# Attention and two feed-forward blocks on one core: a seven-product scheme in all four matrix layers, with running sums seeded in PSUM

## The chip, the cores and the metric

The kernel runs on one core of a Trainium2 chip, as one launch. The metric is the device time in microseconds; the median of several runs counts. The core has five engines that run beside each other: TensorE (PE, matmuls, with its weight loads as PEld), VectorE (DVE), ScalarE (ACT), GpSimd (POOL) and SyncE (SP), which here issues nearly all DMAs. PSUM has eight banks into which TensorE writes; SBUF holds everything else on the core.

## The reference

```python
def _attn_ref(q, k, v, w_pre, w_post):            # 4 batches, 12 heads, 448 rows, 64 wide
    scores = np.matmul(q, k.transpose(0, 1, 3, 2)) / np.sqrt(64)
    scores = np.einsum('bhij,hg->bgij', scores, w_pre)
    attn = softmax over the last axis (with its maximum taken off)
    attn = np.einsum('bhij,hg->bgij', attn, w_post)
    return np.matmul(attn, v)

def _moe_ref(x, w_gate, w_val, w_out):            # x 1792 x 768, d_ff 1536
    gate = 1.0 / (1.0 + np.exp(-(x @ w_gate)))
    return (gate * (x @ w_val)) @ w_out

def _moe2_ref(x, w_in, w_out):                    # d_ff 2048
    h = np.maximum(x @ w_in, 0.0)
    return (h * h) @ w_out
```

The result of the attention, with its heads side by side, is the x of the first block, whose result is the x of the second.

## The kernel before

The attention part comes first and is written out by hand in `attention`. The feed-forward part is made by `mlp`, which lists tasks (a DMA, a split, a job of three matmuls, a sum) with the engines that can run them, the time they are needed by (counted in TensorE jobs) and the buffers they use. `Feed` is a planner: it holds durations for each kind of task and emits the tasks in the order that its own clock gives, some of them between the steps of the attention, the rest after it. The order on each engine is thus fixed when the kernel is built; on the chip each engine works through its own list and waits where data or a buffer isn't there.

The 1792 tokens are handled as two halves of two batches each. A half's activations are two column blocks of 448 tokens (c = 0, 1), and a matrix is cut into tiles of 128 x 128. There are four matrix layers: gv (gate and val together), wo, wi and wo2. The order is gv, wo for the first half, gv, wo for the second, then wi, wo2 for the first and wi, wo2 for the second. Every matrix product is done in higher precision by splitting both operands into a rounded part and a rest (`split`: a cast on ACT, a subtraction on DVE). One `job` multiplies one weight tile with one operand of 128 x 448 in three matmuls, so a layer's work is counted in jobs.

The layers gv and wi take two weight tiles by two in the contraction and in the output, with the two column blocks, as a 2 x 2 block product, and do it in seven products instead of eight (`quad`). `PRODUCTS = ("a1", "b6", "c7", "d5", "a2", "c4", "d3")` gives the order of the products and in which of four PSUM banks each is summed. ACT copies the first product out of its bank, and DVE forms the other running sums from the banks and SBUF buffers (`c`). The layers wo and wo2 are done with all eight products (`plain`): for three output tiles at a time, over the contraction, each weight tile is used for both column blocks, so the six tiles of one weight buffer serve twelve jobs.

Weights come from the host in a compressed 64-bit form. `convert` turns twelve tiles at a time into floats (`raw`: two ACT operations, two DVE operations and two GpSimd adds for each half), forms for gv and wi the three or four block sums of the seven-product scheme (on DVE or GpSimd, whichever the planner finds free) and stores the blocks to DRAM. `Stream.unit` later loads six tiles at a time (`w32`, three buffers) and splits them into `w` (three buffers). `PACE` and `BEFORE` set from which TensorE job on a piece of conversion may be emitted. Operands of gv and wi are loaded, combined and split in `operands`; for wo and wo2 each g tile is split into one of six short-lived buffers (`brief`) right before use.

Of the kernel before, what the change touches and what calls it, by code (L numbers as in the profile page):

```python
# [19 lines left out]
P = 128  # L20
# [11 lines left out]
GT3 = 3  # L32
# [424 lines left out]
BEFORE = 10  # L457
PACE = 44
PRODUCTS = ("a1", "b6", "c7", "d5", "a2", "c4", "d3")


def square_order(KT, MT):

    order = []
    for m in range(0, MT, 2):
        for dm, dk in ((0, 0), (0, 1), (1, 1), (1, 0)):
            order += [(k + dk, m + dm) for k in range(0, KT, 2)]
    return order


def plain_order(KT, MT):

    return [(k, m + i) for m in range(0, MT, GT3) for k in range(KT) for i in range(GT3)]

# [24 lines left out]
class Feed:  # L499
# [122 lines left out]
    def emit(self, at, t, o):  # L622
# [5 lines left out]
        if t.size:  # L628
            self.wire = max(self.wire, end) + t.size / 250e3
            end = self.wire + self.land  # L630
# [56 lines left out]
def mlp(ctx, tc, xs, wg, wv, wo, wi2, wo2, out):  # L687
# [10 lines left out]
    tiles = {"wg": wg, "wv": wv, "wo": wo, "wi2": wi2, "wo2": wo2}  # L698
    K1, K2 = wg.shape[0] * UT // KD, wi2.shape[0] * UT // KD
    W = UT * P  # L700
    H3 = KD // 2
    BL = H3 * P

# [14 lines left out]
    def after_mixes():  # L718
# [3 lines left out]
        feed.stock(xts, pool("m_x1", 1, side="left"), 1)  # L722
        feed.stock(banks, pool("m_ps0", 6, space=PSUM, side="left"), 6)

    def after_all():
# [3 lines left out]
        feed.stock(cs, pool("m_c", 2, side="left"), 2)  # L729
# [6 lines left out]


    pace = [-BEFORE]

    def convert(key, src, n, square, dst, need):  # L740

        hold = max(0, min(pace[0] * PACE, need))
        pace[0] += 1

        y = Buf(ys, [P, 8 * BL], F32, "y")

        def t(*a, **kw):
            feed.task(*a, **kw).hold = hold

        for h in range(2):  # L750
            raw = Buf(raws, [P, W, 2], U32, "raw")
            part = [(y, b) for b in ((0, 4), (5, 7))[h]] if square else [(y, 4 * h), (y, 4 * h + 1)]

            def at(h=h, y=y):
                v = y.tile.bitcast(U32)
                if square:
                    v = v.rearrange("p (b e) -> p b e", e=BL)
                    return v[:, (0, 5)[h] : (5, 8)[h] : (4, 2)[h]]
                return v[:, h * W : (h + 1) * W]

            def of(ap):
                return ap.rearrange("p (b e) -> p b e", e=BL) if square else ap

            def load(e, i, h=h, raw=raw):
                v = src[2 * n + h].bitcast(U32).rearrange("p (m t) -> p m t", t=2)
                e.dma_start(out=raw.tile[:, i * BL : (i + 1) * BL], in_=v[:, i * BL : (i + 1) * BL])

            def bias(e, raw=raw):
# [378 lines left out]
```

## Time and profile before

| | before |
|---|---|
| median of three runs | 1429.9 us |
| the runs | 1419.75, 1429.9, 1431.61 us |
| the profiled execution, its time and its span | 1432.88 and 1431.2 us |
| TensorE busy, matmuls | 1380.3 us (96%), 7848 |
| DVE, ACT, POOL busy | 1041.0 (73%), 699.1 (49%), 333.1 us (23%) |
| DMA | 259.85 MB, 182 GB/s |

The time is that of the whole execution on the device, the span runs from its first to its last instruction. Busy shares add up neither over engines nor over stages: an engine that idles may still be the one that is waited for.

### The profile page before, as it was taken

The page shows a single profiled execution, that of the slowest core. Times are in us where ns is not written, and L with a number is a line of the kernel's source. Part 1 is how long each engine was busy: PE and PEld are TensorE (multiplying, and loading weights), DVE is VectorE, ACT ScalarE, POOL GpSimd, SP SyncE. Part 2 cuts the span into 40 slices and gives each one's busy share as a digit, 9 for nine tenths or more (in the row PEclk, how much of TensorE's full clock was granted, in tenths as well). Part 3 has the DMA queues.
Part 4 walks back from the last instruction along what each step waited for, and adds up shares of the span by engine and source line. Part 5 has one row for each costly group of instructions (what it writes and reads, how often), then busy time and mean ns, then how long its engine had stood idle before and what let it go on. Part 6 is the DMA issues. An engine that isn't in the chain of part 4 may idle for free.

```text
span 1431.2 us, 22572 instructions
## 1 busy us (share of the span) xinstructions
PE 1380.3 (96%) x7848; PEld 1113.8 (78%) x7848; DVE 1041.0 (73%) x1864; ACT 699.1 (49%) x1312; POOL 333.1 (23%) x356
## 2 busy tenths in 40 slices
PE   6889998999999899999999999999999999999999
PEld 2445555565665689999898999999899999999998
DVE  2767777797797787789767778987879854666442
ACT  2444445455555544446654455566445644233353
POOL 3243443343352032131124222022212100000000
PEclk9999999999999999999999999999999999999999
DMA  5757868868768256655665666377665433333121
GB/s 152 209 187 213 243 184 250 246 197 256 236 188 274 90 189 225 221 178 172 209 231 191 231 229 207 99 266 261 217 192 167 167 106 103 103 109 88 56 83 39
DMA packets 123342, 259.85 MB, mean 182 GB/s; under 512 B 16156, under 2 KB 62684, under 8 KB 123228
## 3 DMA queue, kind: packets, MB, share of 16 engines
q1 hardware_dynamic: 122848, 257.83, 57.2%
q8 instruction: 62, 1.02, 0.3%
q10 hardware_dynamic: 380, 0.57, 0.1%
q14 instruction: 52, 0.43, 0.1%
HBM read 163.74 MB, written 55.05 MB: 153 GB/s over the span
## 4 chain that ended last, share of the span: by engine, by line
PE 85%; DMA 7%; DVE 5%; ACT 1%; issue 1%; POOL 1%; SPq 0%; DVEq 0%; POOLq 0%; ACTq 0%
PE ps L886 64%; PE ps_p L283 8%; PE ps_s L202 5%; PE ps_v L312 4%; PE ps_m L238 4%; DMA g<-e 4%; DMA vraw<-in_v 2%; DVE ap L295 1%; DVE nm L249 1%; DVE e L212 1%; DMA t<-xs 1%; DVE s L874 0%; DVE w L874 0%; POOL wn L267 0%; ACT e L214 0%
## 5 line engine op out<-in xcount | busy, mean ns | idle before, releaser
L886 PE MATMUL ps<-s,w 128*128 128x448 f32 x4536 | 933.0, 367 | 6.4 <-DVE s L874 3.1
L886 PEld LDWEIGHTS ps<-s,w 128*128 128x128 f32 x4536 | 851.9, 188 | 87.5 <-DVE s L874 5.7
L797 POOL TENSOR_TENSOR y<-y,raw 128x384 int32<-128x384 int32 x136 | 161.6, 1205 | 528.1 <-DVE y L781 171.0
L871 ACT CAST w<-w 128x768 fp32r<-128x768 f32 x196 | 163.3, 835 | 181.8 <-PE ps L886 155.1
L283 PEld LDWEIGHTS ps_p<-wn,a 128*112 128x112 f32 x1440 | 158.7, 178 | 89.2 <-POOL wn L267 38.6
L874 DVE TENSOR_TENSOR w<-w,w 128x768 fp32r<-128x768 f32 x196 | 207.4, 1061 | 26.7 <-ACT w L871 23.1
L874 DVE TENSOR_TENSOR s<-g,s 128x448 fp32r<-128x448 f32 x224 | 152.9, 699 | 99.2 <-ACT s L871 98.8
L871 ACT CAST s<-g 128x448 fp32r<-128x448 f32 x224 | 126.5, 567 | 166.5 <-PE ps L886 159.9
L283 PE MATMUL ps_p<-wn,a 128*112 128x120 f32 x1440 | 183.9, 276 | 11.9 <-POOL wn L267 5.5
L900 DVE TENSOR_TENSOR c<-ps,c 128x448 f32<-128x448 f32 x200 | 124.4, 622 | 90.3 <-PE ps L886 86.8
L267 POOL TENSOR_SCALAR wn<-wq,sm 128x120 f32<-128x120 f32 x166 | 115.3, 695 | 272.6 <-DVE sm L264 207.7
L249 DVE TENSOR_REDUCE nm<-ps_m 128x1 f32<-128x448 f32 x180 | 111.1, 617 | 54.0 <-PE ps_m L238 53.9
L256 ACT ACTIVATE a<-ps_m,nm 128x448 f32<-128x448 f32 x180 | 114.5, 636 | 57.1 <-DVE sm L261 45.6
L295 DVE COPY ap<-ps_p 112x480 f32<-112x480 f32 x180 | 114.4, 649 | 14.2 <-PE ps_p L283 12.8
L202 PE MATMUL ps_s<-k,q 64*120 64x448 f32 (+1 forms) x384 | 108.5, 627 | 15.3 <-ACT e L214 9.7
L214 ACT COPY e<-ps_s 120x448 f32<-120x448 f32 (+1 forms) x96 | 51.1, 532 | 130.3 <-PE ps_s L202 87.5
L238 PE MATMUL ps_m<-g,wp 64*64 64x448 f32 x720 | 93.5, 580 | 5.1 <-DMA g<-e 5.1
L212 DVE COPY e<-ps_s 120x448 f32<-120x448 f32 (+1 forms) x96 | 60.0, 625 | 50.9 <-PE ps_s L202 28.5
L312 PEld LDWEIGHTS ps_v<-ap,vraw 112*64 112x64 f32 x768 | 52.7, 137 | 49.7 <-ACT xo L327 13.7
L312 PE MATMUL ps_v<-ap,vraw 112*64 112x240 f32 (+1 forms) x768 | 82.7, 360 | 8.6 <-DMA vraw<-in_v 7.1
L202 PEld LDWEIGHTS ps_s<-k,q 64*120 64x120 f32 (+1 forms) x384 | 31.0, 184 | 61.5 <-ACT a L256 20.4
L908 ACT COPY c<-ps 128x448 f32<-128x448 f32 x88 | 46.5, 533 | 52.0 <-PE ps L886 49.3
(40 smaller groups left out, 684.2 us busy)
## 6 DMA issues: line engine op xcount, KB each, us to landing
w<-gv SPq DMA_DIRECT2D x84, 384.0 KB
g<-e SPq DMA_DIRECT2D x132, 210.0 KB
raw<-in_wo SPq DMA_DIRECT2D x56, 384.0 KB
w<-wo SPq DMA_DIRECT2D x56, 384.0 KB
w<-wi SPq DMA_DIRECT2D x56, 384.0 KB
gv<-y SPq DMA_DIRECT2D x36, 384.0 KB
raw<-in_wi SPq DMA_DIRECT2D x32, 384.0 KB
vraw<-in_v SPq DMA_DIRECT2D x48, 224.0 KB
```

The source lines that it names most:

```text
L202: nc.tensor.matmul(ps[o][:isz], lhsT=q_t[n][r, p, :isz], rhs=kt[r], start=True, stop=True)
L238: nc.tensor.matmul(ps[u * HP : (u + 1) * HP], lhsT=wp[r], rhs=g_t[n][r, 2 * t + u], start=True, stop=True,)
L249: nc.vector.tensor_reduce(out=nm, in_=ps, op=ALU.max, axis=AX.X, negate=True)
L267: nc.gpsimd.tensor_scalar(out=wn, in0=wq, scalar1=sm, scalar2=None, op0=ALU.mult)
L283: nc.tensor.matmul(ps[:JP, jt], lhsT=a[:, jt * JP : (jt + 1) * JP], rhs=wn.rearrange("p g i -> p (g i)"), start=True, stop=True,)
L295: nc.vector.tensor_copy(ap[c][:, :, :, g0 - i0 : g0 - i0 + rows], ps[:JP, :, :, :rows])
L312: nc.tensor.matmul(ps[o * D : (o + 1) * D, :w], lhsT=vraw[c, (h + o) // HV][:, (h + o) % HV, jt, :], rhs=ap[c][:, jt, h + o, :w], start=jt ...
L797: e.tensor_tensor(out=y3, in0=y3, in1=c3, op=ALU.add)
L871: e.copy(dst.tile[:, 0], src.tile)
L874: e.tensor_tensor(out=dst.tile[:, 1], in0=src.tile, in1=dst.tile[:, 0].bitcast(F32), op=ALU.subtract)
L886: e.matmul(bank.tile, lhsT=a[k], rhs=x[l], start=start and n == 0, stop=stop and n == 2, skip_group_check=more,)
L900: e.tensor_tensor(out=out.tile, in0=a.tile, in1=b.tile, op=op)
```

## The change

The layers wo and wo2 are now done in seven products as well (`deep`), over all pairs of the contraction for one product before the next is begun, for the three pairs of output tiles at once. All their weights have to be in place, as seven blocks instead of four, when the layer begins, and a weight buffer of six tiles serves six jobs. The subtractions of the scheme on the operand side are done on g tiles in SBUF (`first`, and in `deep`).

In all four layers the products come in another order, 1 5 6 2 7 3 4, and the running sums are kept in PSUM: when product 1 is done ACT copies its bank a into bank b, and product 6 is added to it by its matmuls; then b is copied into c, and products 7 and 4 are added there, and 3 is added into b. `wide` (gv, wi) runs two such quads side by side (gate and val, or two pairs of outputs), `deep` three. So that matmuls add to what ACT has written, `prime` lets a matmul write each of the eight banks once before the first layer.

The dependencies of a job on the cast and on the rest of a split are now kept apart. The planner's conversion pacing changes (`BEFORE`, `FAST`, `PACE`), it counts 330 instead of 250 bytes per ns for DMAs, there are three `c` buffers instead of two and twelve `t` buffers instead of thirteen, and converted blocks are stored in pieces of 1536 instead of up to 3072 bytes for each partition.

```diff
-BEFORE = 10
-PACE = 44
-PRODUCTS = ("a1", "b6", "c7", "d5", "a2", "c4", "d3")
+BEFORE = 11
+FAST = 22
+PACE = 36
+PRODUCTS = ("1a", "5d", "6b", "2a", "7c", "3b", "4c")
+SUMS = ((1, 7, 6, ALU.add), (2, 1, 0, ALU.subtract), (4, 0, 7, ALU.subtract), (5, 3, 2, ALU.subtract))
...
+    def prime(w, slot):
+
+        b = [Buf(banks, [P, N], F32, "ps") for _ in range(8)]
+
+        def run(e):
+            for x in b:
+                e.matmul(x.tile, lhsT=w[0].tile[:, 0, :P], rhs=slot.tile[:, 0], start=True, stop=True)
...
+    def quads(count, jobs, then):
+
+        a, d, b, c = ([Buf(banks, [P, N], F32, "ps") for _ in range(count)] for _ in range(4))
+        bank = {"a": a, "b": b, "c": c, "d": d}
+        p5, v = {}, {}
+        for n, (name, k) in enumerate(PRODUCTS):
+            jobs(n, name, bank[k], name in "15")
             now = len(feed.jobs)
...
+            for i in range(count):
+                if name == "1":
+                    activate(b[i], a[i], now - 1)
+                elif name == "5":
+                    p5[i] = temp()
+                    activate(p5[i], d[i], now)
+                elif name == "6":
+                    activate(c[i], b[i], now)
+                elif name == "2":
+                    then(i, 0, 0, a[i], now)
+                elif name == "7":
+                    v[i] = temp()
+                    tt(v[i], c[i], p5[i], ALU.add, now, False)
+                    then(i, 1, 1, v[i], now)
+                elif name == "3":
+                    tt(p5[i], b[i], p5[i], ALU.add, now, False)
+                    then(i, 0, 1, p5[i], now)
+                else:
+                    then(i, 1, 0, c[i], now)
...
+    def wide(stream, hf, pair, slot, then):
+
+        def jobs(n, name, bank, fresh):
+            for i in range(2):
+                for q in range(H3):
+                    w = stream.tile(hf, pair * PAIR + (2 * n + i) * H3 + q, len(feed.jobs))
+                    job(bank[i], w, slot[name, q], fresh and q == 0, q == H3 - 1, fresh)
+
+        quads(2, jobs, then)
+
+    def deep(stream, hf, g, then):
+
+        pairs = stream.pairs
+
+        def jobs(n, name, bank, fresh):
+            for j in range(pairs):
+                k = 2 * j
+                b11, b12, b21, b22 = g[k, 0], g[k, 1], g[k + 1, 0], g[k + 1, 1]
+                now = len(feed.jobs)
+                if name == "6":
+                    tt(b12, b22, b12, sub, now)
+                elif name == "7":
+                    tt(b11, b12, b11, sub, now)
+                elif name == "4":
+                    tt(b21, b21, b12, sub, now)
+                src = {"1": b11, "5": b12, "6": b12, "2": b21, "7": b11, "3": b22, "4": b21}[name]
+                s = Buf(brief, [P, 2, N], F32R, "s")
+                split(src, s, N, now)
+                for i in range(H3):
+                    w = stream.tile(hf, (n * pairs + j) * H3 + i, len(feed.jobs))
+                    job(bank[i], w, s, fresh and j == 0, j == pairs - 1, fresh)
+
+        quads(H3, jobs, then)
...
-    def plain(stream, hf, KT, g, then):
-
-        for m0 in range(0, KD, GT3):
...
-                for i in range(GT3):
-                    w = stream.tile(hf, (m0 * KT + k * GT3) + i, len(feed.jobs))
-                    for c in range(2):
-                        if k == 0:
-                            bank[i, c] = Buf(banks, [P, N], F32, "ps")
-                        job(bank[i, c], w, s[c], k == 0, k == KT - 1)
...
+    def first(g, p):
+        k = 2 * p
+        tt(g[k, 1], g[k, 1], g[k, 0], sub, len(feed.jobs) + 60)
```

Three places of the order show what moves. The names are the program's: `w` is a split weight buffer, `s` a split operand, `g` the gated or squared values, `t` operands of the next layer, `c` sums in SBUF, `ps` banks, `raw` and `y` conversions.

TensorE's list, from the end of the attention part on, before and then in the change:

```order
L238 MATMUL ps_m<-g_147,wp 64x448 x4
L283 MATMUL ps_p<-wn,a 112x120 x8
L238 MATMUL ps_m<-g_147,wp 64x448 x2
L283 MATMUL ps_p<-wn,a 112x120 x16
L312 MATMUL ps_v<-ap,vraw 64x208 x48
L886 MATMUL ps<-s,w 128x448 x4536
```

```order
L237 MATMUL ps_m<-g_135,wp 64x448 x4
L282 MATMUL ps_p<-wn,a 112x120 x8
L237 MATMUL ps_m<-g_135,wp 64x448 x2
L282 MATMUL ps_p<-wn,a 112x120 x16
L311 MATMUL ps_v<-ap,vraw 64x208 x48
L921 MATMUL ps<-s,w 128x448 x8
L903 MATMUL ps<-s,w 128x448 x4284
```

The attention part ends alike; eight priming matmuls are new, and 4284 matmuls of the layers stand where 4536 stood.

DVE's list in the first wo layer, from its third weight split on, before and then in the change (the number tells buffers apart):

```order
L874 TENSOR_TENSOR w_6856<-w32_6785,w_6856 128x768
L874 TENSOR_TENSOR s_6763<-t_5510,s_6763 128x448
L900 TENSOR_TENSOR t_5510<-t_5554,t_5510 128x448
L900 TENSOR_TENSOR t_6917<-t_5565,t_5510 128x448
L874 TENSOR_TENSOR s_6915<-g_6145,s_6915 128x448
L874 TENSOR_TENSOR s_6926<-g_6181,s_6926 128x448
L874 TENSOR_TENSOR w_6932<-w32_6799,w_6932 128x768
L874 TENSOR_TENSOR s_6938<-t_6917,s_6938 128x448
L900 TENSOR_TENSOR t_5554<-t_5565,t_5554 128x448
L874 TENSOR_TENSOR s_6953<-g_6166,s_6953 128x448
L874 TENSOR_TENSOR s_6959<-g_6137,s_6959 128x448
```

```order
L891 TENSOR_TENSOR w_6962<-w32_6874,w_6962 128x768
L891 TENSOR_TENSOR s_6971<-g_6850,s_6971 128x448
L891 TENSOR_TENSOR s_6981<-g_5717,s_6981 128x448
L928 TENSOR_TENSOR g_5717<-g_5689,g_5717 128x448
L928 TENSOR_TENSOR g_6929<-g_6929,g_6850 128x448
L928 TENSOR_TENSOR g_5632<-g_5717,g_5632 128x448
L891 TENSOR_TENSOR w_7003<-w32_6919,w_7003 128x768
L891 TENSOR_TENSOR s_7009<-g_5948,s_7009 128x448
L891 TENSOR_TENSOR s_7015<-g_6192,s_7015 128x448
L928 TENSOR_TENSOR g_5948<-g_5919,g_5948 128x448
L928 TENSOR_TENSOR g_6192<-g_6157,g_6192 128x448
```

Between two weight splits stand two operand splits and two or three subtractions on g, where before stood operand splits and operands of the next layer; each of these weight buffers now serves half as many jobs.

DVE's list in the wi layer of the first half, between its 21st and 22nd weight split (before, from the 19th on, and then in the change):

```order
L874 TENSOR_TENSOR w<-w_10351,w 128x768
L776 TENSOR_SCALAR y<-raw 128x768
L781 SCALAR_TENSOR_TENSOR y<-raw,y 128x768
L900 TENSOR_TENSOR g<-ps,g 128x448
L900 TENSOR_TENSOR c<-ps,c 128x448 x2
L1036 SCALAR_TENSOR_TENSOR g<-c 128x448 x2
L874 TENSOR_TENSOR w<-w_10389,w 128x768
L776 TENSOR_SCALAR y<-raw 128x768
L874 TENSOR_TENSOR w<-w_10414,w 128x768
L900 TENSOR_TENSOR c<-ps,c 128x448
L781 SCALAR_TENSOR_TENSOR y<-raw,y 128x768
L900 TENSOR_TENSOR c<-ps,c 128x448
```

```order
L891 TENSOR_TENSOR w<-w_10485,w 128x768
L809 TENSOR_TENSOR y<-y 128x384 x4
L1097 SCALAR_TENSOR_TENSOR g<-c 128x448 x2
L928 TENSOR_TENSOR c<-ps,c 128x448
L779 TENSOR_SCALAR y<-raw 128x2x384
L782 SCALAR_TENSOR_TENSOR y<-raw,y 128x2x384
L928 TENSOR_TENSOR c<-ps,c 128x448
L779 TENSOR_SCALAR y<-raw 128x768
L782 SCALAR_TENSOR_TENSOR y<-raw,y 128x768
L891 TENSOR_TENSOR w<-w_10558,w 128x768
```

Four block sums and four conversion steps now stand between two weight splits, where one conversion step stood.

## Rows read from the trace of the kernel before

**Rows 1.** The page's parts 1 and 2: busy time, and the granted clock in 40 slices.

```profile
PE 1380.3 (96%) x7848; PEld 1113.8 (78%) x7848; DVE 1041.0 (73%) x1864; ACT 699.1 (49%) x1312; POOL 333.1 (23%) x356
...
PEclk9999999999999999999999999999999999999999
```

**Rows 2.** The page's part 4: the chain that ended last, by line.

```profile
PE ps L886 64%; PE ps_p L283 8%; PE ps_s L202 5%; PE ps_v L312 4%; PE ps_m L238 4%; DMA g<-e 4%; DMA vraw<-in_v 2%; DVE ap L295 1%; DVE nm L249 1%; DVE e L212 1%; DMA t<-xs 1%; DVE s L874 0%; DVE w L874 0%; POOL wn L267 0%; ACT e L214 0%
```

**Rows 3.** The page's part 5: groups, busy us, mean ns, idle before.

```profile
L886 PE MATMUL ps<-s,w 128*128 128x448 f32 x4536 | 933.0, 367 | 6.4 <-DVE s L874 3.1
...
L900 DVE TENSOR_TENSOR c<-ps,c 128x448 f32<-128x448 f32 x200 | 124.4, 622 | 90.3 <-PE ps L886 86.8
...
L908 ACT COPY c<-ps 128x448 f32<-128x448 f32 x88 | 46.5, 533 | 52.0 <-PE ps L886 49.3
```

**Rows 4.** Chain in order of time: start us, us, what.

```profile
488.32 3.86 PE ps L886 x18
...
1011.18 416.50 PE ps L886 x2014
```

**Rows 5.** Timeline of ACT in the second gv layer.

```profile
817.14 0.84 ACT L871 CAST w<-w 128x768 fp32r<-128x768 f32 x1 [2.81 <-PE ps L886]
...
846.33 0.84 ACT L871 CAST w<-w 128x768 fp32r<-128x768 f32 x1 [1.29 <-PE ps L886]
```

**Rows 6.** Timeline of ACT in the last wi layer.

```profile
1241.70 0.84 ACT L871 CAST w<-w 128x768 fp32r<-128x768 f32 x1 [1.31 <-PE ps L886]
...
1275.18 0.84 ACT L871 CAST w<-w 128x768 fp32r<-128x768 f32 x1 [2.46 <-PE ps L886]
```

**Rows 7.** Windows, the layers' start: busy PE, PEld, DVE, ACT, POOL; PEclk, DMA, GB/s.

```profile
488.25:504.96 16.71, 13.60 (x60) 10.27 (x58) 12.87 (x24) 13.32 (x24) 0.00 (x0) 1.00 0.45 133
```

**Rows 8.** Timeline of TensorE in the second gv layer.

```profile
756.49 4.05 PE L886 MATMUL ps<-s,w 128*128 128x448 f32 x12 [1.97 <-DVE w L874]
```

**Rows 9.** Windows around the same place.

```profile
754.50:756.50 2.00, 0.03 (x2) 0.01 (x1) 2.00 (x3) 0.53 (x1) 1.89 (x2) 1.00 0.03 11
756.50:760.50 4.00, 4.00 (x13) 3.59 (x14) 3.96 (x4) 0.00 (x0) 3.92 (x3) 0.62 0.83 249
```

**Rows 10.** Timeline of ACT around the same place.

```profile
743.21 0.84 ACT L871 CAST w<-w 128x768 fp32r<-128x768 f32 x1 [2.81 <-PE ps L886]
...
752.56 2.47 ACT L871 CAST w<-w 128x768 fp32r<-128x768 f32 x3
```

**Rows 11.** Groups by form, whole run: conversion steps, squares and block sums on DVE.

```profile
L781 DVE SCALAR_TENSOR_TENSOR y<-raw,y 128x768 uint32<-128x768 uint32 x68 | 64.9, 954 | 1.2
...
L776 DVE TENSOR_SCALAR y<-raw 128x768 uint32<-128x768 uint32 x68 | 43.2, 635 | 3.6 <-ACT raw L770 3.5
...
L1036 DVE SCALAR_TENSOR_TENSOR g<-c 128x448 f32<-128x448 f32 x48 | 30.3, 639 | 1.3
...
L815 DVE TENSOR_TENSOR y<-y 128x384 f32<-128x384 f32 x44 | 24.5, 565 | 0.1
```

**Rows 12.** Groups on DVE in 894.5 to 983.4 us (second wo layer).

```profile
L874 DVE TENSOR_TENSOR s<-g,s 128x448 fp32r<-128x448 f32 x45 | 33.5, 766 | 8.5 <-ACT s L871 8.3
L874 DVE TENSOR_TENSOR w<-w,w 128x768 fp32r<-128x768 f32 x14 | 14.1, 1005 | 2.4 <-ACT w L871 2.2
...
L900 DVE TENSOR_TENSOR t<-t 128x448 f32<-128x448 f32 x9 | 5.5, 620 | 0.1
```

**Rows 13.** Groups on DVE in 1309 to 1431 us (last wo2 layer, GpSimd idle).

```profile
L874 DVE TENSOR_TENSOR s<-g,s 128x448 fp32r<-128x448 f32 x61 | 37.8, 625 | 54.5 <-ACT s L871 54.5
L874 DVE TENSOR_TENSOR w<-w,w 128x768 fp32r<-128x768 f32 x15 | 14.4, 958 | 1.5
```

**Rows 14.** Windows: the second wo layer.

```profile
894.50:983.40 88.90, 88.90 (x441) 82.40 (x440) 74.68 (x106) 53.83 (x92) 16.23 (x13) 1.00 0.59 200
```

**Rows 15.** Windows with much DMA traffic.

```profile
930.00:966.00 36.00, 36.00 (x179) 33.37 (x179) 29.46 (x39) 22.37 (x37) 9.21 (x8) 1.00 0.74 264
...
940.00:960.00 20.00, 20.00 (x100) 18.55 (x99) 17.25 (x22) 11.44 (x19) 5.27 (x5) 1.00 0.89 324
```

More of the change, by code (lines that the diff above doesn't have):

```diff
@@ L702, in mlp @@
     BL = H3 * P
+    PAIR = 14 * H3
     def pool(name, bufs, **kw):
@@ L750, in convert @@
         for h in range(2):
[L751 to L762, printed above, removed]
@@ L852, in unit @@
[L852 to L866 removed]
+            keys = []
@@ L874, in rest, with job @@
             e.tensor_tensor(out=dst.tile[:, 1], in0=src.tile, in1=dst.tile[:, 0].bitcast(F32), op=ALU.subtract)
-        feed.task(high, [act(n)], need, reads=[src], writes=[dst])
-        feed.task(rest, [dve(n)], need, reads=[src], writes=[dst])
-    def job(bank, w, slot, start, stop, more=False):
+        feed.task(high, [act(n)], need, reads=[src], writes=[(dst, 0)])
+        feed.task(rest, [dve(n)], need, reads=[src, (dst, 0)], writes=[(dst, 1)])
+    def job(bank, w, slot, start, stop, fresh):
         w, i = w
@@ L900, in run @@
             e.tensor_tensor(out=out.tile, in0=a.tile, in1=b.tile, op=op)
-        feed.task(run, [dve(N, port)], need, reads=[k for k in (a, b) if k is not out], writes=[out])
+        return feed.task(run, [dve(N, port)], need, reads=[k for k in (a, b) if k is not out], writes=[out])
     def activate(out, a, need, func=None):
@@ L1065, in put @@
-    def put(dst, key, m, n0, b):
-        def run(e):
-            e.dma_start(out=dst[m * P : (m + 1) * P, n0 : n0 + N], in_=b.tile)
-        feed.task(run, [SP], len(feed.jobs), reads=[b], writes=[key] if key else [], size=P * N * 4)
-    gv = Stream("gv", [wg, wv], True)
-    so = Stream("wo", [wo], False)
-    si = Stream("wi", [wi2], True)
-    s2 = Stream("wo2", [wo2], False)
+                    feed.task(run, [dve(N)], now + 6, reads=[b], writes=[o])
+            wide(stream, hf, p, slot, then)
@@ new lines, in squared, with store, then, run @@
+            first(g, 2 * p)
+            first(g, 2 * p + 1)
+        return g
+    def store(dst, key, n0):
+        def then(i, r, c, b, now):
+            m = 2 * i + r
+            if b.stock is banks:
+                o = temp()
+                activate(o, b, now + 2)
+                b = o
+            def run(e):
+                at = n0 + c * N if key is None else 0
+                d = dst if key is None else dst[c]
+                e.dma_start(out=d[m * P : (m + 1) * P, at : at + N], in_=b.tile)
+            feed.task(run, [SP], now + 4, reads=[b], writes=[key(c, m)] if key else [], size=P * N * 4)
+        return then
```

334 lines of the change are left out of this document (157 added, 177 removed).

## The prediction

> **What bounds the kernel now.** I read the share of busy time first, and then only the chain of waits, since a busy share is an average over stages. TensorE is busy for 1380.3 of 1431.2 us and its clock is granted in full throughout [rows 1]. The chain that ended last runs for 64% through one line, L886, the matmuls of the four feed-forward layers [rows 2]. These 4536 matmuls stand for 933.0 us, and TensorE waited only 6.4 us for other engines ahead of them [rows 3]. They begin at 488.32 us and end at 1011.18 + 416.50 = 1427.7 us [rows 4], which is 939.4 us, two thirds of the span. In this stretch a matmul that is not issued is time that is not spent, as long as the other engines keep up. So the two questions are how many matmuls go away, and whether DVE, ACT and the DMA still keep up.
>
> For the price of a matmul I don't take the mean duration of a row, because matmuls overlap. In the timeline of ACT each weight split waits for TensorE to free a buffer, and a buffer serves six jobs of three matmuls. From 817.14 to 846.33 us eight such steps pass, 144 matmuls in 29.19 us, 0.2027 us each [rows 5]. From 1241.70 to 1275.18 us nine pass, 162 in 33.48 us, 0.2067 each [rows 6]. So there are two paces, 2% apart. The first half of the layers (792 jobs, 2376 matmuls) costs 2376 x 0.2027 = 481.6 us, the second (720 jobs, 2160 matmuls) 446.5, together 928.1. The other 939.4 - 928.1 = 11.3 us were lost: 16.71 - 13.60 = 3.1 us at the start [rows 7], and 8.2 us in a few later places.
>
> One of these shows what a lost place costs. At 756.49 us TensorE had waited 1.97 us for a weight split [rows 8]. It had been idle in nearly all of 754.5 to 756.5, and in the next 4 us the granted clock was 0.62 and 13 matmuls went through instead of 20 [rows 9], another 1.4 us. The cause stands on ACT: between two weight casts, at 743.21 and 752.56, lie 9.35 us of other work [rows 10], where a buffer lasts 3.65.
>
> **The change part by part.**
>
> Matmuls removed: each of the two second layers goes from four block products of eight to seven, that is from 144 to 126 jobs and from 192 to 168, for each half of the batch. That is 2 x 18 x 3 = 108 matmuls at 0.2027 (21.9 us) and 2 x 24 x 3 = 144 at 0.2067 (29.8 us). The eight priming matmuls at the start cost 8 x 0.2027 = 1.6. All of it is on the path: 51.7 - 1.6 = 50.1 us less. The order of TensorE in the attention part is unchanged.
>
> Attention: one more load of raw weights and three more stores are issued before the first layer, among some 300 other DMAs. I take 0, with 3 us to either side; three runs of one kernel lie 12 us apart anyway.
>
> Start of the layers: the priming needs all eight banks, so it waits for ACT's last copy of the attention part, about 0.5 us. Against that, in the first pair of blocks each operand split now serves six jobs instead of three, so the same splits have 3.65 us for each product instead of 1.82. Between none and all of the 3.1 us [rows 7] goes; I take half. Together -1.1 us.
>
> Seeds: before, the running sums were added by DVE out of the banks, five for each quad, 200 at 0.622 us [rows 3]. Now there are 24 wide and deep groups with 156 copies on ACT, 52 of them into an SBUF buffer, at the 0.533 us of the bank copies [rows 3], and 104 sums on DVE. A seed is needed one product after its bank is finished: 18 matmuls, 3.65 us, in the wide layers, and two copies take 1.07. The bank copies of before spent 49.3 us waiting for TensorE [rows 3], so ACT comes early. I cost the seeds at nothing; what hides them is the product in between.
>
> Bursts of conversion work on ACT: the place of [rows 10] has four raw conversions and five short operations between two weight casts; in the changed order no place after the first groups has more than four raw conversions, or more than seven operations in all. Of the 8.2 us of later losses I take half away: -4.1; between 0 and 8.2.
>
> A burst on DVE, new: in the first wi layer the order puts between two weight splits four block sums (0.565), two squares (0.639), two sums out of banks (0.622) and two pairs of conversion steps (0.635 + 0.954) [rows 3, 11]: 2.3 + 1.3 + 1.2 + 3.2 = 8.0, and the split itself 1.0. Ahead of these stand one sum and a split that wait for product 7. So the second split is done 0.6 + 1.0 + 9.0 = 10.6 us after product 7, and TensorE needs it after two products, 7.4. A wait of 3.2, below 2 us only if DVE is early; with the clock 1.4 more. I take 4.4, between 0 and 6. Behind that split wait the next weight loads on SP, which stand behind the stores of the same block sums.
>
> The deep layers, DVE: this is the risk. A weight buffer lasted twelve jobs (7.3 us) there and now lasts six (3.65), so the three buffers cover half the time. In the first wo layer the order has 21 weight splits, 41 operand splits, 33 subtractions and splits of the next operands, 9 sums and 5 conversion steps. At the durations of the same layer before, beside GpSimd (1.005, 0.766, 0.620 [rows 12], 0.622 [rows 3] and 3 x 0.635 + 2 x 0.954 [rows 11]) that is 21.1 + 31.4 + 20.5 + 5.6 + 3.8 = 82.4 us. With splits at the price without GpSimd (0.958 and 0.625 [rows 13]) it is 75.6. TensorE needs 126 x 3 x 0.2027 = 76.6. Before, DVE was busy 74.68 of 88.9 us in the second of these layers [rows 14]. By the order two to three half blocks are converted in the first one instead of six, so GpSimd disturbs less and the lower end is nearer; and DVE may be up to two buffers (7.3 us) behind before TensorE waits. I take 1.5 us for each of the two wo layers and the first wo2 layer, 4.5, between 0 and 17 (what lies over TensorE's time at the upper price, counted in the same way: 5.8, 8.1 and 3.3).
>
> The same rows bear on a rule. An operand split took 0.766 us with GpSimd at work and 0.625 without it [rows 12, 13]. By the Trainium skill, page "SBUF — State Buffer", section "Who interferes with whom", a VectorE operation with two SBUF inputs and a GpSimd operation that reads SBUF block each other for a whole instruction. By that rule the change, which adds 112 such subtractions and more block sums, would pay the upper price; by the rows of the two layers it lies between.
>
> Sum: 1432.9 (the profiled execution) - 50.1 - 1.1 - 4.1 + 4.4 + 4.5 = 1386.5. The profiled execution lies 3.0 above the median of the runs shown, 1429.9, so for a median I say **1385 us**, 3.1% less.
>
> **The rivals.**
>
> DVE becomes the bound in the deep layers. For: the sums of 76 to 82 us against 76.6, and buffers that last half as long. Against: DVE idled for 8 us and more ahead of its operand splits in the same layer before, waiting for ACT [rows 12]. Price 17 us instead of 4.5: 1385 + 12.5 = 1398, and with five falls of the clock at 1.4 us 1405.
>
> The DMA becomes the bound in the wide layers. By the order the second gv layer issues 42 loads and 34 raw blocks of 384 KB, 36 stores and 12 transfers of 224 KB, 45.0 MB in 153 us, 294 GB/s; the first gv layer as much and the first wi layer 29.9 MB in 104 us. If the 264 GB/s of 930 to 966 us [rows 15] were all there is, these three would take 170, 170 and 113 us, 43 us more than TensorE needs: 1428, no change. Against: 940 to 960 us carried 324 GB/s at a share of 0.89 with TensorE busy all the time [rows 15].
>
> Slower than before: the seeds come late. There are 24 groups with two hand-overs from TensorE to ACT and back, 48 in all. If ACT reached them a whole product late, each would cost a wait like that of 756 us, 1.97 + 1.4 = 3.4 us: 1385 + 162 = 1547. It decides from 45 / 48 = 0.9 us for each hand-over on. Against it speaks the ACT idle time of [rows 3]; for it only that seeds share ACT's queue with the raw conversions.
>
> The pace: if all matmuls ran at 0.2067, the result is 9 us higher, 1394; if all ran at 0.2027, 8 lower, 1377. Nothing in the profile shows what sets it, so it goes into the range.
>
> **How the numbers follow.** Forecast with either pace 0.77 (1373 to 1397), DVE bound 0.12 (1398 to 1405), DMA bound 0.05 (1415 to 1432), seeds late 0.03, something better than all of it 0.03. The range of 1373 to 1402 takes the paces, the lower ends of the unknown costs and half of the DVE rival. About 1% is what a measurement of this kernel can tell from no change, that is 1415.6 to 1444.2. Faster by over 1%: 0.77 + 0.12 + 0.03 and a fifth of the DMA case, 0.93. Within 1%: the rest of the DMA case, 0.04. Slower: 0.03.
>
> **What would show it.** Right: 4284 + 8 matmuls of the layers over some 885 to 895 us; the same pace of 0.203 to 0.207; no wait of TensorE for an ACT copy into a bank; a wait of about 3 us for a weight split in the first wi layer, with the granted clock lower behind it; DVE busy 90% and more in the wo layers. Wrong: waits of TensorE for operand splits all through the deep layers (DVE); weight casts on ACT that wait for a DMA in the gv layers (DMA); or attention ending more than 5 us off 488.

## The result, and the profile after

The changed kernel takes 1376.26 us in the median of four runs (1362.63 to 1395.29), the kernel before, run beside it, 1430.63. The ratio is 0.9605, 95% interval 0.9514 to 0.9695; one run of the four, 1395.29 at a lower mean clock, is left out of it. A second set of six runs gave 0.9685 (0.9635 to 0.9734). The profiled execution took 1377.83, 55.1 us less than the one before. Forecast were 1385 and 46.4 us.

The page's parts 1 and 5 of the changed kernel (groups: busy us, mean ns, idle before) answer to [rows 1, 3]:

```profile
PE 1322.3 (96%) x7604; PEld 1067.6 (78%) x7604; DVE 1086.5 (79%) x1953; ACT 764.7 (56%) x1434; POOL 329.3 (24%) x353
...
L903 PE MATMUL ps<-s,w 128*128 128x448 f32 x4284 | 876.9, 367 | 3.8 <-DVE w L891 3.8
```

TensorE's idle time in the layers has shrunk to a single wait, 3.8 us for a weight split. The groups of all engines add that the seeds are copies of 515 ns, ahead of which ACT waited 26.7 us for TensorE, so ACT is still early:

```profile
L936 ACT COPY ps<-ps 128x448 f32<-128x448 f32 x104 | 52.0, 515 | 27.7 <-PE ps L903 26.7
```

The chain in order of time (start, us, what) answers to [rows 4]. The priming starts at 490.36, the last matmul ends at 1032.76 + 339.90 = 1372.66: 882.3 us of layers where there were 939.4.

```profile
481.70 8.66 PE ps_v L311 x96
492.18 532.77 PE ps L903 x2628
1032.76 339.90 PE ps L903 x1636
```

The one wait is the burst on DVE that the prediction placed in the first wi layer. The timeline of DVE shows it between two weight splits, at 1021.87 and 1031.75: four block sums (2.08), two squares, two sums out of banks, and the conversion steps. The only idle time in it, 0.96 us, was spent waiting for ACT.

```profile
1021.33 0.62 DVE L928 TENSOR_TENSOR c<-ps,c 128x448 f32<-128x448 f32 x1 [0.32 <-PE ps L903]
1021.87 1.04 DVE L891 TENSOR_TENSOR w<-w,w 128x768 fp32r<-128x768 f32 x1
1022.84 2.08 DVE L809 TENSOR_TENSOR y<-y 128x384 f32<-128x384 f32 x4
1024.83 1.15 DVE L1097 SCALAR_TENSOR_TENSOR g<-c 128x448 f32<-128x448 f32 x2
...
1027.25 0.96 DVE L782 SCALAR_TENSOR_TENSOR y<-raw,y 128x768 uint32<-128x768 uint32 x1
1028.12 0.62 DVE L928 TENSOR_TENSOR c<-ps,c 128x448 f32<-128x448 f32 x1
1029.70 1.14 DVE L779 TENSOR_SCALAR y<-raw 128x768 uint32<-128x768 uint32 x1 [0.96 <-ACT raw L773]
...
1031.75 0.95 DVE L891 TENSOR_TENSOR w<-w,w 128x768 fp32r<-128x768 f32 x1
```

Windows around the wait (us, TensorE busy, granted clock, DMA) answer to [rows 9]: behind 3.8 idle us the mean granted clock is 0.57 over 4 us, so most of them passed at 1.2 and not at 2.4 GHz, and 12 matmuls went through instead of 20.

```profile
1028.95:1032.75 3.80, 0.04 (x1) 1.00 0.60 220
1032.75:1036.75 4.00, 3.99 (x12) 0.57 0.50 147
```

Windows over the two wo layers and the first wo2 layer (TensorE, its weight loads, DVE, ACT and GpSimd busy, clock, DMA) answer to [rows 14]. DVE is busy for 71 and 73 of 77 us and then for 90 of 104, and TensorE all the time:

```profile
645.00:722.00 77.00, 77.00 (x381) 71.37 (x381) 70.99 (x112) 54.42 (x91) 8.71 (x7) 1.00 0.61 195
...
875.00:952.00 77.00, 77.00 (x381) 71.36 (x380) 72.92 (x112) 52.60 (x89) 10.44 (x6) 1.00 0.59 183
...
1060.00:1164.20 104.20, 104.20 (x506) 94.65 (x505) 90.00 (x142) 63.97 (x110) 0.00 (x0) 1.00 0.49 143
```

### The profile page after: what moved, and what is told of

It reads as the page before. It is cut to its first block, busy times and chain, and to the rows that moved or that the text cites. A ratio compares the mean times of both kernels' runs of the same rounds, so it can differ in the third digit from the quotient of the medians.

```text
span 1376.1 us, 22485 instructions
## 1 busy us (share of the span) xinstructions
PE 1322.3 (96%) x7604; PEld 1067.6 (78%) x7604; DVE 1086.5 (79%) x1953; ACT 764.7 (56%) x1434; POOL 329.3 (24%) x353
## 4 chain that ended last, share of the span: by engine, by line
PE 87%; DVE 5%; DMA 5%; ACT 1%; issue 1%; POOL 0%; SPq 0%; ACTq 0%; DVEq 0%; POOLq 0%
PE ps L903 63%; PE ps_p L282 8%; PE ps_s L201 6%; PE ps_v L311 5%; PE ps_m L237 5%; DMA g<-e 2%; DMA vraw<-in_v 2%; DVE ap L294 2%; DVE nm L248 1%; DVE e L211 1%; DVE y L782 1%; DMA k<-in_k 0%; DVE y L779 0%; ACT e L213 0%; DMA gv<-y 0%
## 5 line engine op out<-in xcount | busy, mean ns | idle before, releaser
L903 PE MATMUL ps<-s,w 128*128 128x448 f32 x4284 | 876.9, 367 | 3.8 <-DVE w L891 3.8
L903 PEld LDWEIGHTS ps<-s,w 128*128 128x128 f32 x4284 | 805.6, 188 | 74.8 <-DVE w L891 4.1
L891 DVE TENSOR_TENSOR w<-w,w 128x768 fp32r<-128x768 f32 x238 | 248.5, 1046 | 95.4 <-ACT w L888 93.8
L888 ACT CAST w<-w 128x768 fp32r<-128x768 f32 x238 | 199.0, 836 | 167.4 <-PE ps L903 147.0
L793 POOL TENSOR_TENSOR y<-y,raw 128x384 int32<-128x384 int32 x136 | 166.9, 1245 | 425.3 <-DVE y L782 127.2
L888 ACT CAST s<-g 128x448 fp32r<-128x448 f32 x196 | 109.9, 566 | 40.5 <-PE ps L903 35.2
L891 DVE TENSOR_TENSOR s<-g,s 128x448 fp32r<-128x448 f32 x196 | 122.0, 633 | 4.6 <-ACT s L888 0.6
L201 PE MATMUL ps_s<-k,q 64*120 64x448 f32 (+1 forms) x384 | 105.1, 615 | 13.1 <-ACT e L213 7.7
L928 DVE TENSOR_TENSOR c<-ps,c 128x448 f32<-128x448 f32 x104 | 63.9, 619 | 10.1 <-PE ps L903 9.4
L773 ACT ACTIVATE raw<-raw 128x768 f32<-128x768 f32 x68 | 62.0, 912 | 11.9 <-DMA raw<-in_wo 5.2
```

Of the source, the lines that this page charges most:

```text
L201: nc.tensor.matmul(ps[o][:isz], lhsT=q_t[n][r, p, :isz], rhs=kt[r], start=True, stop=True)
L793: e.tensor_tensor(out=y3, in0=y3, in1=word(0)[:, i].bitcast(I32), op=ALU.add)
L888: e.copy(dst.tile[:, 0], src.tile)
L891: e.tensor_tensor(out=dst.tile[:, 1], in0=src.tile, in1=dst.tile[:, 0].bitcast(F32), op=ALU.subtract)
L903: e.matmul(bank.tile, lhsT=a[k], rhs=x[l], start=start and n == 0, stop=stop and n == 2, skip_group_check=not fresh,)
```

## The experiments

Twelve runs. All but 2 and 11 are the changed kernel with the edit shown. In runs 1, 3, 5, 6 and 9 the order of all other instructions is that of the changed kernel; in 4, 8, 10 and 12 the edit is one of the plan, so the order differs. "Layers" is the time from the priming to the end of the last matmul.

**1. The matmuls alone.** Each job of three products also multiplies the two low parts, a term that neither kernel has.

```diff
+TERMS = ((0, 0), (0, 1), (1, 0))
+MORE = (*TERMS, (1, 1))
...
+            terms = MORE if getattr(slot, "more", False) else TERMS
...
                 split(src, s, N, now)
+                s.more = name in "524"
```

> The changed kernel with 252 matmuls more: in three of the seven products of the deep layers each job also multiplies the two low parts (a term that neither kernel has), 108 in the wo layers and 144 in the wo2 layers, as many as the change took away; seeds, splits, DMAs and the order of all other instructions stay. If the matmuls alone are the gain: 108 x 0.2027 + 144 x 0.2067 = 51.7 us more than the changed kernel's 1377.8, so 1429.5, level with the kernel before; 1422 if TensorE runs at 0.2027 to the end. If the deep layers hide some other bound behind TensorE (DVE at 92% there), the added matmuls fill time that is lost anyway, and the result is 1415 or less.

Measured: 1428.84 us in the median of ten runs; before, beside it, 1422.45; ratio 1.0044 (1.0014 to 1.0074). The 252 matmuls give the whole gain back, as the first theory said. The profiled run took 1420.94, the expected 1422 of a run whose pace stays at 0.2027 behind the wait; its layers took 926.7 us. The repeat of the changed kernel below (run 7) ran at the same pace and took 876.4, so a matmul in the deep layers is worth (926.7 - 876.4) / 252 = 0.200 us.

**2. The wide layers alone.** Seeds, the new order in gv and wi and the new plan; the deep layers (wo, wo2) as in the kernel before (eight products, its loop and its weight layout).

```diff
-        deep(so, hf, g, store(two, ...
+        plain(so, hf, K1, g, store(two, ...
-    s2 = Deep("wo2", wo2, K2 // 2)
+    s2 = Plain("wo2", wo2, K2 // 2)
```

> One half of the change alone: priming, seeds, the new blocks and the new plan in the wide layers (which had seven products before, too), but the deep layers as in the kernel before, eight products with twelve jobs for each weight buffer; 4536 + 8 matmuls. If the deep layers' matmuls are the gain and seeds are worth nothing by themselves: changed kernel 1377.8 + 51.7 - 5.5 (the DVE burst in the first wi layer and the clock behind it, since fewer block sums stand there) = 1424, or 1417 if the pace stays 0.2027 to the end. If the seeds were what pays: 1400 or less. If they cost something: above 1433.

Measured: 1425.18 (ten runs), ratio 1.0018 (0.9986 to 1.0050): no change. TensorE waited 1.1 us in the layers, 0.9 of it once for a seed. In the profile the layers took 931.3 us, 8.1 less than in the kernel before, with nearly as many matmuls at each pace: the lost places go with this half of the change already. But its last attention matmuls began at 487.49 us, 7.8 later, which takes that back in this profile. Seeds in place of DVE sums, with the new plan, are worth nothing in the time of the whole; the gain comes with the deep layers. Whether these could have their seven products without seeds, no run shows.

**3 and 5. Seeds three and six times over.** The edit of run 3; run 5 has a 6 for the 3.

```diff
-                e.copy(out.tile, a.tile)
+                for _ in range(3 if out.stock is banks else 1):
+                    e.copy(out.tile, a.tile)
```

> Every seed copy from bank to bank is made three times over, the order of all other instructions unchanged: 208 ACT copies more, 107 us of ACT. If the product in between hides the seeds: two banks take 2 x 3 x 0.515 = 3.1 us against 3.65 of the product, so no TensorE wait for a seed, and 0 to 5 us more from places where ACT is full anyway. If the seeds just come in time now, each of 40 hand-overs in the wide layers is 2 us later: 80 us more, 1458.

> Every seed copy from bank to bank six times over, the order of all other instructions unchanged. If the product in between is what hides a seed: in the wide layers two banks take 2 x 6 x 0.515 = 6.2 us against 3.65, a wait of some 2.6 us at each of 40 hand-overs, 104 us, and 1.7 us at half clock behind most of them: 1480 to 1550. In the deep layers three banks take 9.3 us against 18 or 24 jobs (10.9 or 14.6), so there should be next to no wait for a seed there. If what hides a seed is rather that the product behind it can start late, or that ACT has time to spare: below 1420. If pauses draw the pace anew, some of the many stretches between pauses run at 0.2067 and others at 0.2027, in all layers.

Measured, threefold: 1386.64, some 10 us more. Table of what TensorE waited for (us, times, longest):

```profile
PE ps L903 <- DVE w L891: 4.7, 2, 4.5
PE ps L903 <- ACT ps L937: 4.1, 10, 1.1
```

The expectation of no wait for a seed was wrong, by ten waits of 0.4 us. The layers took 884.6 us, 8.2 more than in the repeat of the changed kernel (run 7).

Measured, sixfold: 1502.59, in the range of the first theory, but not by its sum. The same table, and TensorE's timeline over one group of the first gv layer, then in the first wo layer:

```profile
PE ps L903 <- ACT ps L937: 74.4, 60, 5.3
...
PE ps L903 <- DVE w L891: 10.8, 6, 5.4
```

```profile
562.42 2.09 PE L903 MATMUL ps<-s,w 128*128 128x448 f32 x9 [1.28 <-ACT ps L937]
565.60 7.57 PE L903 MATMUL ps<-s,w 128*128 128x448 f32 x36 [1.09 <-ACT ps L937]
574.39 17.00 PE L903 MATMUL ps<-s,w 128*128 128x448 f32 x81 [1.22 <-ACT ps L937]
...
704.68 24.09 PE L903 MATMUL ps<-s,w 128*128 128x448 f32 x108 [3.20 <-ACT ps L937]
```

In the gv layer the waits come in the rhythm of a group of 126 matmuls: 2.4 us in two parts at its first hand-over and 1.2 at its second, where the arithmetic had 2.6 at each. Of the 74.4 us of seed waits 52.4 fell in the wide layers, for which 104 were expected, and 22.0 in the deep ones, for which next to none was; that the total came out in the range is luck in part. In the wo layer the product lasts 11 us and three seeds take 9.3, and still 3.2 us were waited: between the second seed's copies and the third's, ACT's timeline has casts and copies out of banks from 696.69 to 701.35 us, 4.7 us of other work in the same queue. So the cover is the product less what else ACT does in it, and it ends at about three copies for each seed.

**4 and 8. Early weight splits.** A weight split is ranked as if due twelve jobs earlier.

```diff
-        split(w32, w, W, need)
+        split(w32, w, W, need - 12)
```

> The changed kernel with one number more in its planner: the load of a weight buffer is due as before, but its split is ranked as if due twelve jobs earlier, so that conversions and block sums step behind it. By the order no stretch of DVE between two weight splits is over 6.3 us (9.1 before, in the first wi layer). The wait of 3.8 us in the first wi layer should go, and with it 1.7 us at half clock. What the trace shows besides: TensorE starts a matmul every 0.2027 us up to that wait and every 0.2067 behind it, and in the kernel before three of four pauses changed the pace, to and fro. Theory A, a pause draws the pace anew: without the wait the pace of the start stays to the end; at 0.2027 the result is 1377.8 - 5.5 - 1638 x 0.0040 = 1365.7, and if the start happened to draw 0.2067, 1383. Theory B, the slow pace belongs to the layers of the second half of the work: it sets in there without any pause, 1372.3.

> The kernel with early weight splits a second time. Its six runs lay in two heaps, 1365 to 1371 and 1380 to 1386. If the pace that the start draws is the cause, this profile shows either 0.2027 over most of the layers and a time near 1367, or 0.2067 over a long stretch from the start and a time near 1382. If something in the attention part is the cause, a slow run shows its extra time before 491 us. Its median should be 5.5 us below that of the changed kernel.

Measured: 1375.54 (six runs, 1364.93 to 1385.95), ratio 0.9669 (0.9617 to 0.9720), and the second time 1366.72 (1360.49 to 1376.84), ratio 0.9625 (0.9573 to 0.9676). DVE's timeline at the same place: the block sums now stand behind the split, or apart from each other.

```profile
1027.60 1.14 DVE L928 TENSOR_TENSOR c<-ps,c 128x448 f32<-128x448 f32 x2
1028.66 0.94 DVE L891 TENSOR_TENSOR w<-w,w 128x768 fp32r<-128x768 f32 x1
1029.53 1.01 DVE L809 TENSOR_TENSOR y<-y 128x384 f32<-128x384 f32 x2
```

The wait is gone; TensorE waited 0.2 us in all of the layers, which took 870.9 and 871.1 us, and the two profiled runs took 1367.18 and 1366.66, theory A's 1365.7. Theory B falls: the pace stayed at 0.2027 through the layers of the second half but for some 22 us behind the remaining pause of 0.4. Both profiles started at the fast pace, so what makes the upper runs of 1376 to 1386 is not shown. Against the changed kernel in the same set (next run) the medians are 9.4 us apart, but the intervals overlap.

**7. The changed kernel again.**

> The changed kernel as it is, beside the kernel with early weight splits, on one chip. The wait of 3.8 us in the first wi layer is in the order and stays. If pauses draw the pace: the stretch up to it and the stretch behind it each run at 0.2027 or 0.2067, so runs lie between 1371 (both fast) and 1388 (both slow). If the pace belongs to the layer: 0.2027 before and 0.2067 behind it again.

Measured: 1376.11 (six runs, 1371.40 to 1385.65). The wait came again, 3.5 us; behind it the pace stayed fast this time, and the layers took 876.4 us instead of 882.3. Windows of 20 us in the first profile and in this one (matmuls recorded in brackets):

```profile
980.00:1000.00 20.00, 20.00 (x100) 1.00 0.73 240
1060.00:1080.00 20.00, 20.00 (x98) 1.00 0.42 118
```

```profile
980.00:1000.00 20.00, 20.00 (x100) 1.00 0.67 212
1060.00:1080.00 20.00, 20.00 (x100) 1.00 0.40 119
```

**6 and 9. More work for DVE in the deep layers.**

```diff
-            e.tensor_tensor(out=dst.tile[:, 1], ...
+            for _ in range(2 if getattr(dst, "more", False) else 1):
+                e.tensor_tensor(out=dst.tile[:, 1], ...
...
                 split(src, s, N, now)
+                s.more = name in "524"
```

Run 9 has `s.more = name == "5"`.

> In three of the seven products of the deep layers the low part of each operand is computed twice, 84 DVE subtractions of 0.62 us more, the order of all other instructions unchanged: 11.2 us in each wo layer, 14.9 in each wo2 layer. DVE then needs 82.2 and 84.1 us in the wo layers, where TensorE takes 77, and 103.7 of 104 in the first wo2 layer. If DVE is within a few per cent of being the bound there: waits for operand or weight splits in the wo layers of 3 to 12 us together, less what the three weight buffers cover, and some clock behind them: 1383 to 1400. If the DVE share of 92% misleads and there is room: 1378, no wait for DVE in the deep layers. If DVE sets the time already and it does not show as a wait: 52 us more, 1430.

> As the run with twice-computed low parts, but in one of the seven products only: 28 DVE subtractions more, 3.7 us in each wo layer and 5.0 in each wo2 layer, DVE at 74.7 and 76.6 of 77 us in the wo layers and 93.8 of 104 in the first wo2 layer. There, with 82 and 84 us in the wo layers, the price was 21 us. If DVE decides from the point on at which it needs as long as TensorE: no wait beyond that of the first wi layer, 1371 to 1388 by the pace. If it decides earlier (no slack at all left at 92%): a third of the price, waits of 4 to 7 us ahead of the second gv and the first wi layer.

Measured, three products: 1399.00, layers 896.7 us. One product: 1376.69, layers 875.8, no wait but that of the first wi layer. The first theory holds in both, in run 6 by its time and not by the place of its waits, as far as one run of each can show. Of run 6's 20.3 us over the repeat of the changed kernel (run 7), 4.7 are no price of DVE: its first 1169 matmuls ran at 0.2067 and not at 0.2027. Windows over the two wo layers, of run 6 and then of run 9:

```profile
655.00:733.10 78.10, 78.10 (x379) 70.93 (x379) 77.06 (x125) 50.17 (x85) 6.43 (x5) 1.00 0.55 177
891.40:969.00 77.60, 77.14 (x380) 70.92 (x379) 76.61 (x123) 48.07 (x83) 12.57 (x4) 1.00 0.52 162
```

```profile
650.20:726.80 76.60, 76.60 (x379) 70.98 (x379) 73.25 (x117) 54.05 (x91) 8.50 (x7) 1.00 0.59 192
880.20:956.90 76.70, 76.70 (x380) 71.08 (x379) 74.72 (x117) 52.04 (x89) 10.36 (x6) 1.00 0.58 182
```

DVE at 96 and 97% of TensorE's time in run 9 costs nothing, and in run 6, at 99%, TensorE waits only 0.4 us within the wo layers. There DVE ends the layer behind its place in the order, and the debt is paid in the next layers, mostly as waits for a seed. Table of waits, and the timeline of ACT ahead of two of the three late seeds of run 6, in the second gv and in the first wi layer:

```profile
PE ps L904 <- ACT ps L937: 9.0, 3, 3.5
PE ps L904 <- DVE w L892: 4.9, 3, 4.1
```

```profile
743.00 0.57 ACT L888 CAST s<-t 128x448 fp32r<-128x448 f32 x1 [3.21 <-DVE t L929]
743.47 0.95 ACT L937 COPY ps<-ps 128x448 f32<-128x448 f32 x2
...
981.19 0.53 ACT L937 COPY ps<-ps 128x448 f32<-128x448 f32 x1
985.45 0.90 ACT L773 ACTIVATE raw<-raw 128x768 f32<-128x768 f32 x1 [3.73 <-DMA raw<-in_wo]
986.25 0.89 ACT L776 ACTIVATE raw<-raw 128x768 int32<-128x768 uint32 x1
987.04 0.52 ACT L937 COPY ps<-ps 128x448 f32<-128x448 f32 x1
```

At 743.00 the seed copies stood in ACT's queue behind a cast that had waited 3.21 us for a subtraction on DVE, and ahead of the seed wait at 1144.20 a cast had waited 5.96 us for one: these two are DVE's debt, passed on by ACT. In the wi layer raw weights landed late, ACT waited 3.73 us for them, and the second seed copy stood behind that. What made this load late is not shown: SP issued it at 978.63, and its longest wait before that was 4.2 us for GpSimd, ahead of a store.

**10. The planner's old constants.**

```diff
-BEFORE = 11
-FAST = 22
-PACE = 36
+BEFORE = 10
+PACE = 44
...
-            self.wire = max(self.wire, end) + t.size / 330e3
+            self.wire = max(self.wire, end) + t.size / 250e3
...
+        hold = max(0, min((i - BEFORE) * PACE, need))
```

> The changed kernel with the planner's constants of the kernel before (one pace of 44 jobs for a conversion, 250 in place of 330 KB per us). By its order conversions pile up: 15.7 and 25.5 us of DVE beyond a buffer's time stand between two weight splits early in the first wo and the first wo2 layer. If the new constants are a part of the gain: waits for a weight split of some 16 us and 28 us (the pile less what the buffers cover) at these two places, 1376 + 44 = 1420, the most of the gain gone. If the pile runs ahead of its place in time because DVE idles before: 1385 or less.

Measured: 1465.50 in one run, 2.8% above the 1425.40 of the kernel before. Both places and both waits are as the order said (16 and 28 us), early in the first wo and the first wo2 layer. TensorE's timeline, and at the second place ACT's:

```profile
679.07 1.12 PE L902 MATMUL ps<-s,w 128*128 128x448 f32 x2 [13.92 <-ACT w L887]
```

```profile
1142.72 5.58 PE L902 MATMUL ps<-s,w 128*128 128x448 f32 x18 [27.07 <-ACT w L887]
```

```profile
1141.83 0.83 ACT L887 CAST w<-w 128x768 fp32r<-128x768 f32 x1 [6.71 <-DMA w<-wo]
```

The first theory holds, but its sum was half the price: TensorE waited 75.8 us, since shorter waits stand around each place, and the mean granted clock fell from 0.995 to 0.971. What TensorE waited for was the weight cast on ACT. At the first place DVE was busy almost throughout from one weight split to the next, 660.57 to 679.19 us, with operand splits, subtractions and four block sums. At the second the cast had waited 6.71 us for its load besides, which SP issued at 1137.99 behind a store that stood 10.9 us for DVE's block sums: the pile held up the loads too. The seven products need the new plan: with the old constants this one run is slower than the kernel before.

**11. The kernel before with early weight splits.** The same edit in the kernel before.

> The kernel before with the same early rank for its weight splits, nothing else of the change. Its later lost places were 756 us (3.8 us with the clock), 712 and 780 us and two near 1008 us, 6.5 us in all, and 4.9 at the start; by the order no ACT stretch between two weight casts is over a buffer's time by more than 4.3 us, and the one of 9.35 us is gone. If these waits can be had without the seven products: 5 to 8 us less, a ratio of 0.995. If they come back elsewhere: 1.000.

Measured: 1421.15 (ten runs) against 1425.40, ratio 0.9968 (0.9939 to 0.9997), 4 us. In its profile TensorE waited 4.6 us for operand splits, at the start, and only 1.3 in the later places. So some 4 us of the gain could be had without seven products in the deep layers.

**12. Early splits with a conversion less in the attention part.**

```diff
-BEFORE = 11
+BEFORE = 9
-        split(w32, w, W, need)
+        split(w32, w, W, need - 12)
```

> Early weight splits, and BEFORE at 9 instead of 11, so that by the order one conversion less (four DVE steps, its loads and stores) stands in the attention part. In the profiles so far the last attention matmuls began at 479.7 and 473.6 us in two profiles with the old conversions, and at 480.4 to 488.4 in eleven with the new ones, with longer waits for the loads of v (9.4 to 11.8 us against 4.6 to 7.1 in four of each kind looked at) and for DVE (8 against 3). If the amount of conversion work beside attention is the cause: the last attention matmuls begin at 480 or earlier, waits of 5 to 8 and 3 to 6 us, and a median of 1361. If it is the new shape of the loads and stores, whose number hardly changes: 482 to 488 again, and a median of 1367 like that of early splits alone.

Measured: 1373.77 (six runs), ratio 0.9677 (0.9650 to 0.9705). The last attention matmuls began at 479.65 us, but the waits in the attention part are what they were:

```profile
PE ps_v L311 <- DMA vraw<-in_v: 9.6, 3, 5.4
PE ps_p L282 <- DVE ap L294: 7.6, 13, 1.7
```

So one conversion less does not take those waits away, and the start of the last attention matmuls follows something else as well. Run 10 divides them: with the old pacing and the new stores TensorE waited 5.9 us for v, as little as in the kernel before (7.1, and 4.6 in run 11), but 8.2 for DVE. In all twelve profiles with the new conversions that wait is 7.6 to 8.4 us, and in the two with the old ones 3.2 and 2.7. Against early splits alone nothing is won, and in the layers three waits came back.

## Why the prediction was right, step by step

It was right in sign, place and main term; two small terms failed, in the same direction. The layers took 882.3 us, just under the 885 to 895 that it named. The median of 1385 is 1.5 above the prediction's own sum: 1386.5 less the 3.0 by which the profiled execution lay above the median is 1383.5. Against the profiled execution before:

| term | forecast, us | measured, us |
|---|---|---|
| matmuls and priming | -50.1 | -51.4 |
| attention | 0 | +2.0 |
| start of the layers | -1.1 | -4.5 |
| seeds | 0 | 0 |
| later lost places | -4.1 | -7.0 |
| DVE burst, first wi layer | +4.4 | +5.5 |
| DVE in the deep layers | +4.5 | 0 |
| the rest | | +0.3 |
| sum | -46.4 | -55.1 |

**Matmuls.** Right, and shown by runs 1 and 2. Measured is worked out from counts and paces: before, 2426 matmuls at 0.2027 and 2110 at 0.2067, 927.9 us; after, 2648 and 1636 and the priming's 1.6, 876.5. The small excess is the pace: fewer fell into the slow stretch. That the second half ran at the slow pace again, as the sum has it, is luck; in run 7 it did not.

**Start.** Mis-sized. [Rows 7] were read as 3.1 us of idle time, but the 60 matmuls in them are only 12.2 us of work in 16.71, so 4.5 were lost. Afterwards no wait is left there, where I took half. Run 2 has none there either and run 11 still 4.6 us, so it is the new wide layers that took it; that six jobs for each operand split are the reason fits, but no run separates them from the priming and the new plan.

**Seeds.** Right: no wait for a seed in the changed kernel, and worth nothing alone (run 2). The cover is thinner than 1.07 against 3.65 us suggests (runs 3 and 5), because the queue is shared.

**Later lost places.** With the start's 4.5 taken out, 939.4 - 927.9 - 4.5 = 7.0 us had been lost in them, and all of it went. It did not hang on the deep layers' seven products: run 2, without them, waited 1.1 us in all of the layers, and run 11, with nothing changed but the rank of weight splits, 1.3 in the later places.

**DVE burst.** Right in place, releaser and size: 3.8 us of wait for 3.2, and 1.7 of clock for 1.4. Run 4 shows the cause by taking it away.

**Deep layers.** This step failed. I added up mean durations to 75.6 to 82.4 us for the first wo layer, where DVE was busy for 70.99. The durations were right; those of all 112 instructions in that layer of the changed kernel sum to 77.7 us. Its two largest groups:

```profile
L891 DVE TENSOR_TENSOR s<-g,s 128x448 fp32r<-128x448 f32 x39 | 23.4, 620 | 0.5
L891 DVE TENSOR_TENSOR w<-w,w 128x768 fp32r<-128x768 f32 x21 | 20.5, 978 | 4.3 <-ACT w L888 4.1
```

But an instruction on DVE starts before the one ahead of it has ended: in the timeline above the step of 0.96 us at 1027.25 is followed at 1028.12, 0.87 later. In the wo layer 84 of the 112 begin early, by 0.08 us in the mean, and that is the 6.7 us between 77.7 and 70.99. Run 9 shows that DVE would have had room for 28 more over the deep layers, and run 6 that the rival was a real one, a few per cent further on: with 84 more the layers are 20.3 us longer, some 15.6 of it apart from the pace. The upper price for operand splits, which the prediction took from the rule of the Trainium skill ("SBUF — State Buffer", "Who interferes with whom") on VectorE and GpSimd, was not paid, 620 ns against 766: GpSimd was busy for 8.71 of the 77 us. That does not speak against the rule; there was little to interfere with.

**Attention.** +2.0 in the profiled pair, within the 3 allowed, and that is luck. Over twelve profiles with the new conversions its last matmuls start at 479.65 to 488.44 us, 483.9 in the mean, and at 479.67 and 473.63 in the two with the old ones. So the 0 was too low, by some 7 us if two profiles can tell. About 5 of them are the wait for DVE that run 12 lists; what makes DVE late there stays open. Whether this or the pace is why run 1 is slower than the kernel before, although the layers of its profile took less (926.7 against 939.4), no run shows; that profile is of its fastest run.

**DMA.** In the stretch of 960 to 980 us 352 GB/s were carried with TensorE busy all the time, so the rival's 264 was no bound. The window (TensorE, clock, DMA):

```profile
960.00:980.00 20.00, 20.00 (x101) 1.00 0.99 352
```

## What to carry to other kernels

When one engine is busy throughout, count its instructions: 252 of them came to within 3% of their forecast, and all else together moved the time by under 4 us, since gains and losses of up to 7 us each cancelled. Check a planned order for what stands between two deliveries of the same buffer, not for the load of the stage: the same kernel with other constants in its plan was, in one run, 2.8% slower than the kernel without the change. Don't compare a sum of mean durations with a busy time; read how far apart neighbouring instructions start.

## What the hardware showed besides

At a granted clock of 1.00 TensorE has two paces for the same matmul, 0.2067 and 0.2027 us. In the start times, the slow one is a start every 206 or 207 ns; in the fast one the steps run 203, 202, 199, 207, 202. The weight loads beside them last 0.188 us in both. The pace belongs neither to a layer nor to the code: the changed kernel ran its second half at 0.2067 in one profile and at 0.2027 in the next. It holds for tens to thousands of matmuls and mostly changes where TensorE pauses. In the 14 profiles the layers began at the fast pace ten times. Of some 80 pauses of over 0.1 us that came at the fast pace about a quarter were followed by the slow one, and of some 25 that came at the slow pace about four in five by the fast one; most of them stand in run 5. Three times it changed with no pause of over 0.04 us: near 1011 us in the kernel before, and near 1058 in both profiles with early splits. The length of a pause did not tell which: the wait in the first wi layer was followed by the slow pace after 3.8 us in the first profile, and by the fast one after 3.8 in run 1 and 3.5 in run 7. 1636 matmuls at the slow pace take 6.5 us more than at the fast one, and the layers of the two profiles of the changed kernel differ by 5.9 (882.3 and 876.4); all 4284 at one pace or the other would be 17 us apart, an estimate, since no profile ran at the slow pace throughout. So what follows a single pause can cost more than its own length, and by that estimate two runs of one kernel may differ by 1% in this alone. What in a pause sets the pace is open.
